# Query transposes of pairs 9 to 33 moved from DMA to TensorE, the last batch's first-half exponentials allowed behind stage A, and new planner constants

## The chip, the cores and the metric

The kernel runs on one core of one Trainium2 chip. A core has five engines with a queue each: TensorE (PE), VectorE (DVE), ScalarE (ACT), GpSimd (POOL) and SyncE (SP, which here issues nearly all DMAs). The metric is device time in microseconds (us); the time of a kernel is the median of several executions. PE rows come in pairs in the profile: PE is the matmul, PEld the load of its weights.

## The reference, cut to what matters

Stage A is attention with a soft cap, for 8 batches, 12 heads, 448 rows and head size 64. Stage B takes its output, heads side by side, as x (768 wide) and runs causal attention with four experts of head size 64, of which each row uses the two with the larger gate.

```python
scores = cap * tanh((q @ k.T) / sqrt(64) / cap)          # stage A, per head
x      = softmax(scores) @ v                             # 448 x 64, 12 heads -> 448 x 768
logits = x @ w_gate                                      # stage B, per batch
for e in range(4):
    a = softmax(causal((x @ wq[e]) @ (x @ wk[e]).T / sqrt(64)))
    out += weight_of_e_in_top_two * ((a @ (x @ wv[e])) @ wo[e])
```

## The kernel before, in words

**Tiling.** Two heads of a batch make a pair; there are 48 pairs, six to a batch. The key axis is cut into three chunks of 128 (one per head) and a shared chunk that holds the last 64 keys of both heads, so a pair has seven score tiles of 128 keys by 448 queries. The pairs of the last batch (42 to 47) are cut in two halves of 256 and 192 queries, and all first halves come before all second halves; together there are 54 "pieces".

**Stage A, per pair.** SP issues the loads of q, k and v for two pairs at a time into four rotating staging buffers (`load_part`, L271 to L297); a load into a buffer waits for the casts that read it last. POOL casts to 16-bit (`cast`, L342). q and k are then transposed so that the head size lies on the partitions. For pairs 0 to 8 PE does this with matmuls against an identity into PSUM (`a_tr`, L388) and DVE copies the result to the tile `qk` (`a_trev`, L408). From pair `FIRST_D` = 9 on, SP issues two DMA transposes instead, one of q and one of k (`a_trd`, L417, the DMA at L423). The DMA leaves q's columns in another order than the PE path, which `a_fill` (L482) undoes when it reads q, with the test `p >= FIRST_D` at L491. PE "fills" score tiles (L494), ACT takes their tanh into `y` (L505) and then the exponential of a whole piece into `pbuf` (L514). PE multiplies by v (`a_pv`, L518 to L535), DVE divides by the row sums (L541, L542), PE transposes the output (L555), and DVE copies it to `xT` (L568).

**Stage B, per batch.** When six pairs of `xT` are there: the projections of v and the gate (L612), with DVE copies that wait for a POOL memset of two columns of `vs` (L621); the projections of q and k (L716); the gate's masks on DVE and POOL; the score fills (L735) and their exponential on ACT (L742); the causal masks on POOL (L750); the product with v (L771) and its scaling (L789); a transpose (L807) and the output projection (L824). DVE copies its result to `ob` (L838) and SP stores it (L847). There are two `ob` buffers, so a copy can wait for the store of two tiles before. For the last batch (7) stage B is done by halves (`add_last`, L1152): the first half as soon as the first-half pieces are through (fills L1017, exponential `p0L` L1024), the second half at the very end (`tX` L946, fills L1055 to L1066, exponentials L1073 and L1077, output `lwo` L1145).

**Order.** Every engine executes in program order, and that order is made when the kernel is built, by a planner (`Sched`, L24). Each unit of work has an engine, a planned duration, dependencies and a due time; at each step the planner takes the unit that can start first and, among those close together, the one due first (`pick`, L122). A DMA also has a planned landing: `land` bytes at 2.15e5 bytes per us behind the DMAs before it (L107). Stage A's fills and ACT's operations have an order of their own (`next_fill`, L1427): the next fill is taken when a score buffer comes free (there are two, of three and two PSUM banks), and other PE units are put ahead of it if they end in time. `PV` shifts the due time of the P·V units, `TB` that of a batch's stage B, `T0D` that of the last batch's first half. Three further PSUM banks are shared by everything else (`NAUX` = 3). A stage B exponential ("X") takes a score buffer in turn when its inputs are planned to be ready; for the last batch, L1446 holds the last piece's fill back until both X of that batch are placed.

Of the kernel before, what the change touches and what calls it, by code (L numbers as in the profile page):

```python
# [14 lines left out]

DEBUG = False
NAUX = 3
PV = (7.0, 3.5, 0.0)
TB = (4.0, 4.0)
PACE = (1.0, 1.0)  # L20
T0D = 3.0


class Sched:  # L24
# [158 lines left out]
def kernel(  # L183
# [26 lines left out]
    TL = S - KM  # L210
    HALF = 256
    FIRST_D = 9

    WIN = (0, 128, 256, S - 128)
    VW = E * Dh + 2
# [81 lines left out]
            eng.dma_start(t[64 * g : 64 * (g + 1), g : 2 * n : 2, KC, :], s[g])  # L297

    def nbytes(n, which):
        return 2 * n * Dh * 4 * {"q": S, "k": KM, "v": KM}.get(which, TL // 2)  # L300

    ld_of = {}
    FIRST = [
# [6 lines left out]

    def add_load(p, n, w, due, e, deps):
        add(
            ("ld", w, p), e, 0.52, deps, due, load_part, p, n, w,
            nc.scalar if e == "ACT" else nc.sync, land=nbytes(n, w),
        )
        for i in range(n):
            ld_of[p + i, w] = ("ld", w, p)
# [87 lines left out]

    a_tr.ps, a_tr.t = {}, {}

    def a_trev(p, what):  # L408
        if p not in qkt:
            t = hd.tile([128, 1024], f16, name=f"qk_{p}", tag="qk", bufs=8)  # L410
            qkt[p] = (t[:, 0:S], t[:, S : S + 512])
            a_tr.t[p] = t
        lo, hi = {"qk": (0, S + 512), "q": (0, S), "k": (S, S + KM), "t": (S + KM, S + 512)}[what]
        cp = nc.scalar.copy if what == "k" else nc.vector.tensor_copy
        cp(a_tr.t[p][:, lo:hi], a_tr.ps.pop((p, what))[:, lo:hi])

    def a_trd(p, what):  # L417
        if p not in qkt:
            t = hd.tile([128, 1024], f16, name=f"qk_{p}", tag="qk", bufs=8)
            qkt[p] = (t[:, 0:S], t[:, S : S + 512])  # L420
        t = qkt[p][0 if what == "q" else 1]
        src = c16.pop(("q", p)) if what == "q" else c16["k", p]
        nc.sync.dma_start_transpose(  # L423
            out=t.rearrange("x (c p) -> x c p", c=4), in_=src.rearrange("p c h d -> p (c h d)")
        )

    def add_tr(p):
        deps = [("cast", w, p) for w in "qk"]
        if p >= 8:
            deps += [("filled", i) for i in of[p - 8]]  # L430
        due = nomp(p) - (8.0 if p > 3 else 3.5)
        if p == 0:
            for w, d in (("k", "k"), ("q", "q"), ("t", "kt")):
                add(("tr" + w, p), "PE", 0.14 * len(w), [("cast", d, p), ("ident",)], due, a_tr, p,
                    w, take=("tr" + w, p), slack=0.0)
                add(("trev" + w, p), "ACT" if w == "k" else "DVE", 0.4, [("tr" + w, p)], -50.0,
                    a_trev, p, w, give=("tr" + w, p))
            add(("trev", p), "-", 0.0, [("trevk", p), ("trevq", p)], -50.0, lambda: None)
            add(("tr", p), "-", 0.0, [("trt", p)], -50.0, lambda: None)
            return  # L440
        if p >= FIRST_D:
            due -= 6.0
            for w in "qk":
                add(("trd" + w, p), "SP", 1.2, [("cast", w, p)] + deps[2:], due, a_trd, p, w,
                    land=160000)
            add(("trev", p), "-", 0.0, [("trdq", p), ("trdk", p)], 0.0, lambda: None)
            add(("tr", p), "-", 0.0, [("trev", p)], 0.0, lambda: None)
            return
        add(("tr", p), "PE", 0.42, deps + [("ident",)], due, a_tr, p, take=("tr", p))
        add(("trev", p), "DVE", 0.58, [("tr", p)], due + 0.5, a_trev, p, "qk", give=("tr", p))  # L450
# [31 lines left out]
    def a_fill(i, slots, sc, tails):  # L482
        p, lo, n = pieces[i]
        qt, kk = qkt[p]
        for at, g, c in slots:
            if (c == KC) != tails:
                continue
            o = sc[:, at, 0:S] if n == S else sc[:, at // 2, at % 2 * 256 : at % 2 * 256 + n]
            r = slice(0, 128) if c == KC else slice(64 * g, 64 * g + 64)
            qs = qt[r, lo : lo + n]  # L490
            if p >= FIRST_D:  # L491
                o = o.rearrange("p (m c t) -> p m c t", c=QC, t=16)
                qs = qt[r, :].rearrange("p (c m t) -> p m c t", c=QC, t=16)[:, lo // 64 : (lo + n) // 64]
            nc.tensor.matmul(o, kk[r, 128 * c : 128 * (c + 1)], qs, start=True, stop=True)  # L494
# [75 lines left out]
    def add_pv(i):  # L570
        p, lo, n = pieces[i]
        b, j = divmod(p, HP)
        last = i == NK - 1
        due = -1000.0 if last else nom[i] + (PV[0] if n == S else PV[1] if lo == 0 else PV[2])
        for u in groups(i):
            for m in range(2):
                d = [("E", i), ("cast", "v", p)]
                d += [("pv", i, u, 0)] if m else []
                d += [("xt", i - 4)] if i >= 4 else []
                add(  # L580
                    ("pv", i, u, m), "PE", 0.26, d, due, a_pv, i, u, m,
                    take=("pv", i, u) if m == 0 else None, slack=0.05,
                )
            add(
                ("pvev", i, u), "DVE", 0.55, [("pv", i, u, 1)], due, a_pvev, i, u,
                give=("pv", i, u),
            )
        d = [("pvev", i, u) for u in groups(i)] + [("perm",)]
        add(("xt", i), "PE", 0.058 * 2 * len(groups(i)), d, due + 1.0, a_xt, i, take=("xt", i),
            slack=0.05 if last else None)  # L590
        d = [("xt", i)]
        if b >= 2:
            d += [("proj", b - 2)]
        add(("xtev", i), "DVE", 0.3 if n == S else 0.2, d, due + 1.0, a_xtev, i, give=("xt", i),
            alt=True)
# [255 lines left out]
    def add_wo(b, n, due, deps):  # L851
        if b < LB:
            deps = deps + stores[-2:-1]
        for f in range(2):
            add(("wo", b, n, f), "PE", 0.34, deps, due, b_wo, b, n, f, take=("wo", b, n, f))
            d = [("wo", b, n, f)]
            add(("woev", b, n, f), "DVE", 0.47, d, due + 0.5, b_woev, b, n, f,
                give=("wo", b, n, f), alt=True)
        add(
            ("st", b, n), "SP", 0.5, [("woev", b, n, 0), ("woev", b, n, 1)], due, b_store, b, n, 0,  # L860
            2, nc.sync, land=1 << 17,
        )
        if b < LB:
            stores.append(("st", b, n))
# [287 lines left out]
    def add_last():  # L1152
# [56 lines left out]
        for j in range(NDC):  # L1209
            for r in range(2):  # L1210
                for w in "qk":
# [1 line left out]
                    d += [("lqk", 1, r, w, j - 1)] if j else []  # L1213
                    d += [("lqk", 1, r, "q", 0)] if w == "k" and j == 0 else []
                    add(
                        ("lqk", 1, r, w, j), "PE", 0.085, d, c + r if j == NDC - 1 else tE - 1.0,
                        l_qk, 1, r, w, j, j + 1, slack=0.05,
                    )
        for r in range(2):
# [7 lines left out]
        for r in range(2):  # L1227
            for i in (1, 0):
                d = [("lqkev", 1, r, w) for w in "qk"] + [("T", NK - 1, 1), ("lqkev", 0, r, "k")]
                if r == 1 and i == 0:  # L1230
                    d += [("lqkev", 1, rr, w) for w in "qk" for rr in range(2)]
                add(
# [16 lines left out]
        for n in (2, 3):  # L1249
# [6 lines left out]
            for f in range(2):  # L1256
# [2 lines left out]
                add(("woev", b, n, f), eng, 0.5, d, c + n, b_woev, b, n, f, f == 1)  # L1259
                add(  # L1260
                    ("st", b, n, f), "SP" if f == 0 else "ACT", 0.4, [("woev", b, n, f)], c + n,
                    b_store, b, n, f, f + 1, nc.sync if f == 0 else nc.scalar, land=1 << 16,
                )

    tail_par = {}
# [161 lines left out]
    def next_fill():  # L1427
        nf, i = state["nf"], state["piece"]
        if i >= NK:
            sch.next_fill = None  # L1430
            return None
        r, armed = tile_free(nf)
        t = max(r, sch.free["PE"])
        if state["x"]:
# [1 line left out]
            d = x_deps(*x)  # L1436
            dur = 0.2 if x[0] == LB else 0.88
            if all(k in sch.done and sch.done[k][0] + 0.2 <= t for k in d) and (
                t + dur + 0.2 <= sch.act_ahead() or i >= NK - 1
                or t > max(sch.done[k][0] for k in d) + 6.0  # L1440
            ):
                return dict(r=r, dur=dur, armed=armed, special=True, go=lambda s: go_x(x, s, dur))
        p, lo, n = pieces[i]
        if ("trev", p) not in sch.done:
            return None
        if i == NK - 1 and info[i]["reads"] == 0 and state["x"]:  # L1446
            return None
        r = max(r, sch.done["trev", p][0] + 0.05)
        one = dict(r=r, dur=0.4, armed=armed, special=True, go=lambda s: go_t([i], s))
        if nf < 1 or n < S or not info[i]["rem"]:  # L1450
            return one
        nxt = pairs_of(i, 1)
        if nxt is None or pieces[nxt[0]][2] < S:
            return one
        r2, armed2 = tile_free(nf + 1)
        r2 = max(r2, nxt[1])
        two = dict(
            r=max(r, r2), dur=0.75, armed=armed and armed2, special=True,
            go=lambda s: go_t([i, nxt[0]], s),
        )  # L1460
        if r2 <= max(r, sch.free["PE"]) + 0.05:
            return two
        if max(r, r2) + 0.75 + sch.LAT["PE"] + 0.25 <= sch.act_ahead():
            return two
        return one

    def tile_of(par):
        return ps_score.tile(
# [143 lines left out]
```

## Time and profile before

| what | us |
|---|---|
| median of 11 runs | 337.95 (335.53 to 342.45) |
| the profiled execution, its own time | 342.45 |
| its span, first to last instruction | 340.7 |
| ACT busy | 293.8 |
| PE busy (ends modelled) | 275.7 |
| DVE busy | 200.4 |
| POOL busy | 174.2 |
| SP: 39 DMA transposes of q and 39 of k, issue of one (median) | 1.23 and 1.22 |
| stores of `ob`, issue to landing (median) | 2.7 |

The profile is of one execution, the slowest of the eleven. Rows name a line, an engine, an operation and its tiles (out<-in). In the list of waits a row says which engine and line sat idle, for which work, for how long in all, how often, and the longest. A timeline row has the start, the time taken, the engine and line, the tiles, how many instructions are merged in it and, in brackets, the idle time of the engine before it and what ended it. SPq is SP issuing a DMA. Busy shares are averages over stages with different limits, so idle time is read where it falls. PEclk is the granted clock of PE, as a part of full speed.

### The profile page before, as it was taken

To read this page: it belongs to the slowest core of one execution; us is meant where nothing else is said; L and a number is where in the kernel's file an instruction comes from. 1 tells how busy PE (TensorE), PEld (TensorE's weight loads), DVE (VectorE), ACT (ScalarE), POOL (GpSimd) and SP (SyncE) were. 2 spreads that over 40 slices of the span, in tenths; PEclk is the share of its full clock that TensorE was granted. 3 is DMA by queue.
4 is the path that set the end of the run, shared out by engine and by line. 5 is a ranking of instruction groups with operands and counts; after the bars stand their busy time and mean duration, and the time that the engine had idled before them with its cause. 6 is when DMAs were issued, how large, how long until landed. Compare 5 with 4: busy or idle time off the path is not lost.

```text
span 340.7 us, 8025 instructions
## 1 busy us (share of the span) xinstructions
PE 275.7 (81%) x3019; PEld 174.8 (51%) x3019; DVE 200.4 (59%) x643; ACT 293.8 (86%) x247; POOL 174.2 (51%) x346
## 2 busy tenths in 40 slices
PE   6767769977699759886799878887879979998972
PEld 2445445654456425454556545454545655576741
DVE  3453325767275835758367374747656647766873
ACT  4899978999799996998689989997988999994661
POOL 5796584895259631964419824673406421074110
PEclk9596769999999998999879999999989999999999
DMA  6999999959899688779799997877762000300035
GB/s 165 251 208 237 236 215 193 194 127 191 207 234 170 159 242 213 153 204 206 190 226 174 188 252 211 223 144 200 187 189 54 2 0 16 133 17 3 18 139 170
DMA packets 105191, 55.74 MB, mean 164 GB/s; under 512 B 65792, under 2 KB 101760, under 8 KB 105152
## 3 DMA queue, kind: packets, MB, share of 16 engines
q1 hardware_dynamic: 93888, 53.06, 67.7%
q0 software_dynamic: 10512, 1.58, 6.8%
q10 hardware_dynamic: 752, 0.59, 0.7%
q8 instruction: 24, 0.39, 0.5%
q14 instruction: 15, 0.12, 0.2%
HBM read 36.19 MB, written 11.01 MB: 139 GB/s over the span
## 4 chain that ended last, share of the span: by engine, by line
DMA 30%; PE 24%; POOL 11%; SPq 10%; DVE 9%; ACT 8%; issue 6%; POOLq 0%; DVEq 0%; ACTq 0%
DMA kst<-in_k_dram 10%; DMA vst<-in_v_dram 7%; DMA qf<-in_q_dram 7%; DMA out_dram<-ob 5%; PE sc L494 5%; PE vps L612 4%; SPq L297 3%; SPq L423 3%; ACT pbuf L514 3%; ACT y L505 3%; PE pv L532 3%; POOL k L351 2%; DVE ob L838 2%; PE wops L824 2%; SPq L288 2%
## 5 line engine op out<-in xcount | busy, mean ns | idle before, releaser
L505 ACT ACTIVATE y<-sc 128x896 f16<-128x896 f32 (+3 forms) x150 | 144.2, 1031 | 24.9 <-PE sc L494 24.4
L514 ACT ACTIVATE pbuf<-y 128x3136 f16<-128x3136 f16 (+2 forms) x54 | 137.8, 2551 | 0.2 <-PE pv L532 0.2
L494 PE MATMUL sc<-qk 64*128 64x448 f16 (+5 forms) x378 | 67.7, 360 | 5.3 <-ACT y L505 3.2
L532 PE MATMUL pv<-v,pbuf 128*128 128x65 f16 x1152 | 63.3, 198 | 0.0
L527 PE MATMUL pv<-v,pbuf 128*128 128x130 f16 x192 | 44.2, 230 | 23.3 <-ACT pbuf L514 13.4
L532 PEld LDWEIGHTS <-pbuf 128*128 128x128 f16 x1152 | 55.1, 101 | 5.1 <-issue 2.6
L347 POOL CAST q<-qf 112x512 f16<-112x512 f32 x46 | 28.3, 615 | 46.8 <-DMA qf<-in_q_dram 35.2
L542 DVE TENSOR_TENSOR xk<-pv,rc 128x256 f16<-128x256 f32 x96 | 40.8, 425 | 3.3
L838 DVE COPY ob<-wops 128x384 f32<-128x384 f32 (+1 forms) x56 | 29.5, 555 | 21.8 <-DMA out_dram<-ob 14.9
L494 PEld LDWEIGHTS <-qk 64*128 64x128 f16 (+1 forms) x378 | 20.3, 95 | 40.4 <-issue 32.3
L357 POOL CAST v<-vst 128x512 f16<-128x512 f32 x48 | 29.2, 619 | 21.5 <-PE pv L532 15.9
L527 PEld LDWEIGHTS <-pbuf 128*128 128x128 f16 x192 | 19.2, 100 | 34.2 <-ACT pbuf L514 18.7
L541 DVE RECIPROCAL rc<-pv 128x4 f32<-128x4 f32 x96 | 17.1, 178 | 27.7 <-PE pv L532 26.9
L824 PE MATMUL wops<-wo,oT 128*128 128x384 f16 x120 | 28.3, 341 | 5.6 <-DVE ob L838 3.4
L660 POOL COPY mb<-mk 128x1024 f16<-128x1024 f16 x14 | 14.2, 1041 | 34.1 <-DVE mk L655 34.1
L612 PE MATMUL vps<-wvg,xT 128*128 128x260 f16 x168 | 30.2, 292 | 1.8 <-DVE ob L838 1.8
L351 POOL CAST k<-kst 128x512 f16<-128x512 f32 x46 | 28.2, 616 | 4.6 <-DMA kst<-in_k_dram 3.7
L568 DVE COPY xT<-xtp 128x448 f16<-128x448 f16 (+2 forms) x52 | 18.8, 364 | 13.8 <-PE xtp L555 13.7
L716 PE MATMUL kps<-xT,wk 128*128 128x448 f16 x84 | 22.4, 353 | 1.8 <-DVE ob L838 1.5
L555 PE MATMUL xtp<-perm,xk 128*128 128x128 f16 x144 | 18.5, 227 | 5.8 <-DVE xk L542 2.6
L750 POOL TENSOR_SCALAR_AFFINE_SELECT pS<-pS 128x128 f16<-128x128 f16 (+1 forms) x56 | 14.6, 281 | 14.7 <-ACT pS L742 13.3
L716 PE MATMUL qps<-xT,wq 128*128 128x448 f16 x84 | 21.9, 358 | 0.1
(164 smaller groups left out, 406.2 us busy)
## 6 DMA issues: line engine op xcount, KB each, us to landing
qf<-in_q_dram SPq DMA_DIRECT2D x22, 448.0 KB, 5.9
vst<-in_v_dram SPq DMA_DIRECT2D x23, 384.0 KB, 5.0
out_dram<-ob SPq DMA_DIRECT2D x23, 384.0 KB, 2.7
kst<-in_k_dram SPq DMA_DIRECT2D x22, 384.0 KB, 4.3
out_dram<-ob SPq DMA_DIRECT2D x8, 192.0 KB, 2.7
kst<-in_k_dram SPq DMA_DIRECT2D x47, 32.0 KB, 4.9
vst<-in_v_dram SPq DMA_DIRECT2D x47, 32.0 KB, 4.6
kst<-in_k_dram SPq DMA_DIRECT2D x4, 192.0 KB, 4.1
```

Source lines behind the costliest of these rows:

```text
L351: cp(c16["k", p][:, 0:n], src.rearrange("p h c d -> p c h d")[:, 0:n])
L357: cp(v16[p % NV][:, :, :, 0:Dh], src)
L494: nc.tensor.matmul(o, kk[r, 128 * c : 128 * (c + 1)], qs, start=True, stop=True)
L505: nc.scalar.activation(ytile[i][:, first : first + nb, :], src, AF.Tanh, scale=isc / capf)
L514: nc.scalar.activation(ptile[i], ytile.pop(i), AF.Exp, scale=capf)
L527: nc.tensor.matmul(pv[:, n, :, :], ptile[i][:, idx[0, KC], w : w + 128], v16[p % NV][:, :, KC, :], start=(n == 0), stop=False, skip_group_ ...
L532: nc.tensor.matmul(pv[:, n, g, :], ptile[i][:, idx[g, c], w : w + 128], v16[p % NV][:, g, c, :], start=False, stop=(c == KC - 1), skip_gro ...
L542: nc.vector.tensor_tensor(xk, pv[:, :, :, 0:Dh], rc.broadcast_to((128, 2, 2, Dh)), ALU.mult)
L612: nc.tensor.matmul(ps, xT[b][:, j, w : w + 128], wvg[:, j, :], start=(j == 0), stop=(j == NDC - 1),)
L716: nc.tensor.matmul(s[which, r], w2[r][:, j, :], xT[b][:, j, :], start=(j == 0), stop=(j == NDC - 1),)
L824: nc.tensor.matmul(ps, s["oT"][:, r, w : w + 128], wo2[r][:, f * (D // 2) : (f + 1) * (D // 2)], start=(r == 0), stop=(r == 1),)
L838: cp(s["ob", n][lo:128, f * (D // 2) : (f + 1) * (D // 2)], s.pop(("wops", n, f))[lo:128, :],)
```

## The change

1. A second bound, `FIRST_Q` = 34, is added. For pairs 9 to 33 only k is transposed by DMA; q is transposed by four PE matmuls into a shared PSUM bank and copied to `qk` by DVE. From pair 34 on both go by DMA as before. `a_fill` undoes the column order from pair 34 on.
2. The planner's numbers: loads, transposes and stores get other planned landing times (a load's issue 0.62 instead of 0.52, a store's landing 1.2 instead of 0.61 us); `PV`, `TB` and `T0D` change; the last three pieces' P·V comes first of all (`LATE`).
3. The last batch's two first-half exponentials may follow stage A: the hold at L1446 goes, an X that wasn't placed by the end is added by `late_x` behind the last piece, and the second-half fills wait for both X. The second-half projections `lqk` get due times by chunk.
4. Two fills of half pieces (`n < S`) may be joined in one step, as those of whole pieces were.

```diff
-PV = (7.0, 3.5, 0.0)
-TB = (4.0, 4.0)
+PV = (9.0, 5.0, 2.0)
+TB = (0.0, 0.0)
 PACE = (1.0, 1.0)
-T0D = 3.0
+LATE = 3
+T0D = -4.0
...
     FIRST_D = 9
+    FIRST_Q = 34
...
     def nbytes(n, which):
-        return 2 * n * Dh * 4 * {"q": S, "k": KM, "v": KM}.get(which, TL // 2)
+        t = {"q": 224 * 0.055, "k": 256 * 0.045, "v": 256 * 0.045}.get(which, 64 * 0.03)
+        return n * t / 16 * 2.15e5
...
-            ("ld", w, p), e, 0.52, deps, due, load_part, p, n, w,
+            ("ld", w, p), e, 0.62, deps, due, load_part, p, n, w,
...
         if p >= FIRST_D:
-            due -= 6.0
-            for w in "qk":
-                add(("trd" + w, p), "SP", 1.2, [("cast", w, p)] + deps[2:], due, a_trd, p, w,
-                    land=160000)
+            for w in "qk" if p >= FIRST_Q else "k":
+                add(("trd" + w, p), "SP", 1.2, [("cast", w, p)] + deps[2:], due - 6.0, a_trd, p, w,
+                    land=1.05 * 2.15e5)
+            if p < FIRST_Q:
+                add(("trq", p), "PE", 0.21, [("cast", "q", p)] + deps[2:], due, a_tr, p, "q",
+                    take=("trq", p))
+                add(("trdq", p), "DVE", 0.37, [("trq", p)], due + 0.5, a_trev, p, "q",
+                    give=("trq", p))
...
-            if p >= FIRST_D:
+            if p >= FIRST_Q:
                 o = o.rearrange("p (m c t) -> p m c t", c=QC, t=16)
...
-        due = -1000.0 if last else nom[i] + (PV[0] if n == S else PV[1] if lo == 0 else PV[2])
+        due = -1000.0 + i if i >= NK - LATE else nom[i] + (PV[0] if n == S else PV[1] if lo == 0 else PV[2])
...
-            2, nc.sync, land=1 << 17,
+            2, nc.sync, land=1.2 * 2.15e5,
...
-                        ("lqk", 1, r, w, j), "PE", 0.085, d, c + r if j == NDC - 1 else tE - 1.0,
+                        ("lqk", 1, r, w, j), "PE", 0.085, d, c + r if j == NDC - 1 else c + 20.0 + j,
...
                 d = [("lqkev", 1, r, w) for w in "qk"] + [("T", NK - 1, 1), ("lqkev", 0, r, "k")]
+                d += [("X", LB, rr) for rr in range(2)]
...
         if i >= NK:
             sch.next_fill = None
+            for x in state["x"]:
+                late_x(x[1])
+            state["x"] = []
             return None
...
-                t + dur + 0.2 <= sch.act_ahead() or i >= NK - 1
-                or t > max(sch.done[k][0] for k in d) + 6.0
+                t + dur + 0.2 <= sch.act_ahead() or t > max(sch.done[k][0] for k in d) + 6.0
...
-        if i == NK - 1 and info[i]["reads"] == 0 and state["x"]:
-            return None
...
-        if nf < 1 or n < S or not info[i]["rem"]:
+        if nf < 1 or (not info[i]["rem"] and n == S):
             return one
...
-        if nxt is None or pieces[nxt[0]][2] < S:
+        if nxt is None or pieces[nxt[0]][2] != n:
             return one
...
+        both = 0.75 if n == S else 0.2 + n / 600
...
+    def late_x(r):
+
+        d = x_deps(LB, r) + [("T", NK - 1, 1)] + [("X", LB, 0)] * r
+
+        def fill():
+            L["late", r] = ps_score.tile(
+                [128, CAPS[tail_par[1]], 512], f32, name=f"lx_{r}", tag=f"sc{tail_par[1]}"
+            )
+            l_fill0(r, L["late", r])
+
+        add(("lfx", r), "PE", 0.45, d, -3000.0, fill)
+        add(("X", LB, r), "ACT", 0.7, [("lfx", r)], -3000.0, lambda: l_exp0(r, L.pop(("late", r))))
```

More of the change, by code (lines that the diff above doesn't have):

```diff
@@ L406, with qk_tile @@
     a_tr.ps, a_tr.t = {}, {}
+    def qk_tile(p):
+        if p not in qkt:
+            t = a_tr.t[p] = hd.tile([128, 1024], f16, name=f"qk_{p}", tag="qk", bufs=8)
+            qkt[p] = (t[:, 0:S], t[:, S : S + 512])
+        return a_tr.t[p]
     def a_trev(p, what):
[L409 to L412, printed above, removed]
+        t = qk_tile(p)
         lo, hi = {"qk": (0, S + 512), "q": (0, S), "k": (S, S + KM), "t": (S + KM, S + 512)}[what]
         cp = nc.scalar.copy if what == "k" else nc.vector.tensor_copy
-        cp(a_tr.t[p][:, lo:hi], a_tr.ps.pop((p, what))[:, lo:hi])
+        cp(t[:, lo:hi], a_tr.ps.pop((p, what))[:, lo:hi])
     def a_trd(p, what):
-        if p not in qkt:
-            t = hd.tile([128, 1024], f16, name=f"qk_{p}", tag="qk", bufs=8)
-            qkt[p] = (t[:, 0:S], t[:, S : S + 512])
+        qk_tile(p)
         t = qkt[p][0 if what == "q" else 1]
@@ L1261, in add_last @@
                     ("st", b, n, f), "SP" if f == 0 else "ACT", 0.4, [("woev", b, n, f)], c + n,
[L1262 removed]
+                    b_store, b, n, f, f + 1, nc.sync if f == 0 else nc.scalar, land=0.6 * 2.15e5,
                 )
@@ L1456, in next_fill @@
         r2 = max(r2, nxt[1])
+        both = 0.75 if n == S else 0.2 + n / 600
         two = dict(
-            r=max(r, r2), dur=0.75, armed=armed and armed2, special=True,
+            r=max(r, r2), dur=both, armed=armed and armed2, special=True,
             go=lambda s: go_t([i, nxt[0]], s),
@@ L1462, in next_fill @@
             return two
-        if max(r, r2) + 0.75 + sch.LAT["PE"] + 0.25 <= sch.act_ahead():
+        if max(r, r2) + both + sch.LAT["PE"] + 0.25 <= sch.act_ahead():
             return two
         return one
+    def late_x(r):
[7 more added lines that the diff above has]
+        add(("X", LB, r), "ACT", 0.7, [("lfx", r)], -3000.0, lambda: l_exp0(r, L.pop(("late", r))))
     def tile_of(par):
```

## The prediction

> **What bounds the kernel now.** I read the page first (which engine is fullest, when), then the waits (what the fullest engine lacks), then ScalarE's timeline with its bracketed idle times, then the other engines around each of these.
>
> ```profile
> span 340.7 us, 8025 instructions
> PE 275.7 (81%) x3019; PEld 174.8 (51%) x3019; DVE 200.4 (59%) x643; ACT 293.8 (86%) x247; POOL 174.2 (51%) x346
> DMA  6999999959899688779799997877762000300035
> ```
>
> ACT is the fullest engine and its order is fixed, so its idle time before the last exponential is lost one for one. The waits say whom it lacks, and who is late behind that:
>
> ```profile
> ACT y L505 <- PE sc L494: 24.4, 20, 3.2
> DVE ob L838 <- DMA out_dram<-ob: 15.9, 10, 4.2
> DVE vs L623 <- POOL vs L621: 6.7, 4, 3.5
> ACT p0L L1024 <- PE sc L1017: 4.5, 1, 4.5
> ```
>
> ACT waits for PE's score fills, 24.4 us. The four before 47 us are 2.6 of it; the sixteen from 47 to 262 us are 21.8. Between 276.7 and 308.3 it never waits over 0.2 us; then come 4.47 us for the last batch's stage B fill (p0L). The largest of the sixteen shows the chain that repeats:
>
> ```profile
> 122.62 1.23 SPq L423 DMA_TRANSPOSE qk<-q  x1
> ...
> 123.95 0.51 SPq L847 DMA_DIRECT2D out_dram<-ob  x1
> ...
> 126.88 1.02 DVE L838 COPY ob<-wops 128x384 f32<-128x384 f32 x2 [3.65 <-DMA out_dram<-ob]
> ...
> 127.49 0.80 PE L824 MATMUL wops<-wo,oT 128*128 128x384 f16 x2 [2.83 <-DVE ob L838]
> ...
> 130.82 0.92 ACT L505 ACTIVATE y<-sc 128x896 f16<-128x896 f32 x1 [3.16 <-PE sc L494]
> ```
>
> A store queues on SP behind a transpose, DVE's next output copy waits for its landing, PE waits for DVE, and the fill behind that on PE is late. The stage table (stretch; busy time and count of PE, weight loads, DVE, ACT, POOL; granted clock, DMA share, GB/s) adds that PE's clock was halved just then:
>
> ```profile
> 127.40:130.80 3.40, 3.31 (x13) 1.54 (x13) 1.93 (x6) 0.25 (x1) 0.00 (x0) 0.50 0.61 118
> ```
>
> Sorted by what PE was held by: stores under DVE's ob copies 9.2 us (130.82, 154.55, 203.20, 233.10, 253.16); stage B's vs memset, which stands on POOL behind a q cast that waits for its load, 4.2 (92.46, 171.17); right after a half-clock stretch 3.7 (163.54, 177.63, 257.12, 260.31); PE simply full or still starting 4.8 (47.54, 54.56, 66.32, 142.47, 246.44).
>
> **What the Trainium skill says.** "TensorE: Matmul & The Clock Gate", Part 1: the clock is halved after an idle window of about 3.4 us, so a PE stall is paid again. The trace agrees: stretches of 3.4 us at 0.50 begin at 127.4, 161.6, 171.8 and 253.7, the first in the 2.83 us wait above. Same page, Part 2: matmuls stay in program order; so does the trace's PE, which lets the fill stand behind the output projection. "DMA: Bandwidth & Descriptors", "Issuing engines are not separate DMA queues": all DMAs share the 16 engines. So fewer transposes help loads and stores too; the trace shows a DMA share of 0.90 from 47 to 165 us and 0.83 from 165 to 262.
>
> **The change part by part.** (1) q of pairs 9 to 33: 25 DMA transposes leave SP, at 1225 ns of issue (median of 39) 30.6 us of that queue, and 25 x 112 x 512 x 2 bytes = 2.9 MB of traffic, at the 192 GB/s of that stretch about 15 us. PE and DVE take over; the row of pair 0 prices it:
>
> ```profile
> L395 PE MATMUL trq<-ident,q x4: 212/213/223, 4.9 to 5.1; 112*128 112x112 f16 x4
> L415 DVE COPY qk<-trq x1: 392/392/392, 5.3 to 5.3; 128x448 f16<-128x448 f16 x1
> ```
>
> 100 matmuls start about 55 ns apart: 25 x 0.22 = 5.5 us of PE (at most 25 x 0.37, the four at half clock at 44.68, = 9.3). DVE gets 25 x 0.392 = 9.8 us; it is 59% busy, so free unless one stands before a copy that PE waits for. PE is the one to pay: of 5.5 us I charge 1.5 to ACT (none if all fall in PE's idle time, all 5.5 if none do). No data is late by this: POOL's casts run 5 to 12 pairs (of about 5.5 us) ahead of use.
>
> (2) Planner numbers. Stores count 1.2 instead of 0.61 us, other landings are re-set; projection dues move 4 us earlier (TB), P·V's 2 us later (PV). This costs no instruction; it moves them. In the built order the output copies no longer straddle as many transposes. What it brings: of the 4.3 us of store stalls at 130.82 and 154.55, where the q transposes also leave, 3.5; of the 4.9 at 203.20 to 253.16, where SP still issues both transposes (pairs 34 on), half, 2.4; of the memset's 4.2, half, 2.1, as the casts ahead of it wait less for loads; of the clock's 3.7, 1.0; of the last 4.8, none. Sum 9.0, net of PE 7.5. Bounds: -6 (below) to 21.8.
>
> (3) Last batch. Now the last piece's fill is held back until both p0L fills are placed:
>
> ```profile
> 307.67 0.67 ACT L505 ACTIVATE y<-sc 128x576 f16<-128x576 f32 x1
> 312.82 1.52 ACT L1024 ACTIVATE p0L<-sc 128x768 f16<-128x768 f32 x2 [4.47 <-PE sc L1017]
> ```
>
> In the changed order the three last pieces run through and p0L follows the last exponential: its end moves from 318.05 by 4.47 + 1.42 to about 312.2. What moves behind it: two exponentials, affine selects, P·V, DVE's scaling, the transposes lot; and PE has lot and otS ahead of the last two P·V windows. After the last exponential: exponentials, gate and a copy 2.0, affine 0.8, P·V 0.35, DVE 0.95, lot 0.3, last P·V 0.6, DVE 0.65, transpose 0.3, copy 0.3 = 6.3 us, where before 318.05 to 322.68 was 4.6: minus 1.7. At the end:
>
> ```profile
> 334.28 1.03 DVE L838 COPY ob<-wops 64x384 f32<-64x384 f32 x2
> ...
> 336.32 0.56 DVE L838 COPY ob<-lwo 64x384 f32<-64x384 f32 x1 [1.01 <-DMA out_dram<-ob]
> ```
>
> These two copies, batch 6's last, now stand before the first lwo copy, in a hole of 0.58 us and the idle time before it, and that batch is ready some 5 us earlier: plus 1.6 (2.0 less 0.4 as ACT's two stores now follow both copies). Sum 5.9 - 1.7 + 1.6 = 5.8. Bounds: 3 (the hole isn't there, the chain is longer) to 8.
>
> (4) Joined half-piece fills, the wait of the second-half fills for p0L, the later lqk dues: nothing. ACT has no idle time at 276.7 to 308.3 to win, a joined fill of seven matmuls (0.5 to 0.7 us) hides under an exponential of 1.32 to 1.74; without that cover 12 x 0.3 = 3.6 us. The second-half fills wait for their own evictions, later than p0L.
>
> The sum against the profiled execution: span 340.7 - 7.5 - 5.8 = 327.4, its time 342.45 - 13.3 = 329.1. But that execution is 4.5 us above the median 337.95, and I take its excess to lie in those stalls: the main part scales by (21.8 - 4.5)/21.8 = 0.79 to 5.9. 337.95 - 5.9 - 5.8 = 326.
>
> **The rivals.** Only the tail pays: casts are pairs ahead, so the transposes were hidden; the stalls are the planner's ordering errors, and new ones replace the old. For it: sixteen different places, only two of them with a q transpose of pairs 9 to 33 just ahead of the store. Against: SP's share in the longest. 337.95 - 5.8 + 1 = 333. That includes the case that (1) does not do what it seems to.
>
> All goes: every stall from 47 us on, and the tail: 337.95 - 17.3 - 6 = 315. For it: ACT would then be at its floor; against: half-clock stretches after 3.4 us of low PE activity are not all due to stores.
>
> Slower: PE takes on a wait for POOL's casts. In the built order the transposes of pairs 9 to 13 stand in the same pair as their casts; the last old PE transpose shows the price:
>
> ```profile
> 44.68 0.37 PE L395 MATMUL tr<-ident,q 112*128 112x112 f16 x4 [3.02 <-POOL q L347]
> ```
>
> PE stood 3.02 us for a cast and ACT lost 1.90 at 47.54. My gain of 11.7 is gone when 6 of the 25 do that; at 10, 326 + 19 = 345. Against: later pairs stand 2 to 6 pairs behind their casts.
>
> No change: the tail pays and six stalls of 1 us come new, 338.
>
> **How the numbers follow.** Forecast 326 at 0.50 (its own range 320 to 331); only the tail, 333, 0.22; all goes, 315, 0.12; slower, 345, 0.10; no change, 338, 0.06. From these: faster by over 0.5% 0.84, within 0.5% 0.06, slower 0.10; 0.5%, 1.7 us, is about what a measurement of this kernel can tell from no change. The range 316 to 337 leaves out the slower case and part of the full recovery.
>
> **What would show it.** The wait of ACT for fills falls from 24.4 to 13 to 17 us, of DVE for out_dram from 15.9 to under 8; DMA share from 47 to 165 us from 0.90 to about 0.8; 39 rows of transposed q become 14; the 4.5 us before p0L vanish; the last exponential ends 20 to 30 us before the span's end. It is wrong if PE waits on POOL q casts for over 5 us after 47 us, or if ACT's sum stays above 22.

## The result, and the profile after

The changed kernel takes 331.87 us (median of 12 runs, 329.41 to 336.32), the kernel before 337.88 (47 runs). The ratio is 0.9819 with a 95% interval of 0.9789 to 0.9848: 6.0 us or 1.8% faster. Medians are of all runs; a ratio compares only those runs of a kernel, and of the kernel before run beside it, that lie within 1.5% of the fastest of their kind, so the two can differ by some tenths of a per cent. The forecast was 326, that is 11.9 us less than before. The profiled execution of the changed kernel took 330.57 us, its span is 328.9. That is 11.8 us less than the span of before, but the execution profiled before lay 4.5 us above its median and this one lies 1.3 us below its own. The two traces therefore show twice what the medians show; below they say where time went, and the medians say how much.

The head of the page of the changed kernel (span; busy time, share and instructions of each engine):

```profile
span 328.9 us, 8178 instructions
PE 278.3 (85%) x3119; PEld 178.5 (54%) x3119; DVE 208.0 (63%) x667; ACT 293.0 (89%) x248; POOL 173.9 (53%) x346
```

ACT is still the fullest engine, with nearly the same busy time (293.8 before), now 89% of a shorter span. The waits (who waited for whom; us in all, times, longest):

```profile
POOL q L350 <- DMA qf<-in_q_dram: 27.7, 8, 8.6
ACT y L513 <- PE sc L502: 15.1, 12, 6.0
...
DVE vs L631 <- POOL vs L629: 6.3, 1, 6.3
```

ACT's wait for fills fell from 24.4 to 15.1 us. DVE's wait for stores, 15.9 before, is no longer in the list. The wait of 4.5 us before `p0L` is gone too. Added up by stage, ACT's bracketed waits for fills are:

| stage, us | before | after |
|---|---|---|
| start to 47 | 2.6 | 5.1 |
| 47 to 75 | 4.0 | 8.5 |
| 75 to 262 | 17.8 | 1.6 |

From 75 us on nearly everything is won, and before 75 us 7.0 us are lost. The stages by engine, first before, then after (stretch; busy time and count of PE, weight loads, DVE, ACT, POOL; clock, DMA share, GB/s):

```profile
47.00:75.00 28.00, 25.66 (x266) 15.68 (x265) 16.14 (x54) 25.40 (x20) 20.80 (x40) 0.90 1.02 177
75.00:165.00 90.00, 71.56 (x808) 45.88 (x806) 55.79 (x168) 81.54 (x61) 50.19 (x91) 0.96 0.86 197
165.00:262.00 97.00, 80.92 (x848) 49.36 (x846) 59.01 (x186) 87.39 (x65) 47.67 (x85) 0.96 0.83 191
```

```profile
47.00:75.00 28.00, 21.77 (x223) 13.84 (x222) 12.65 (x43) 19.49 (x15) 16.82 (x26) 0.82 1.15 215
75.00:165.00 90.00, 80.41 (x958) 52.07 (x956) 63.20 (x200) 89.20 (x67) 56.42 (x108) 1.00 0.81 194
165.00:262.00 97.00, 88.56 (x1015) 56.77 (x1016) 68.20 (x211) 96.21 (x73) 52.08 (x99) 1.00 0.62 152
```

From 75 us on ACT is now busy for 89.2 of 90 and 96.2 of 97 us, and PE's clock shows 1.00. Between 47 and 75 us ACT is busy for only 19.5 of 28 us, where it was 25.4. One stall makes most of that, here in the timeline of the changed kernel:

```profile
47.60 0.98 SPq L281 DMA_DIRECT2D qf<-in_q_dram  x1
...
57.89 0.62 POOL L350 CAST q<-qf 112x512 f16<-112x512 f32 x1 [5.49 <-DMA qf<-in_q_dram]
...
59.70 0.12 POOL L629 MEMSET vs<- 128x6 f16 x1
...
60.43 0.27 PE L535 MATMUL pv<-v,pbuf 128*128 128x130 f16 x1 [5.61 <-DVE vs L631]
...
61.62 0.92 ACT L513 ACTIVATE y<-sc 128x896 f16<-128x896 f32 x1 [5.97 <-PE sc L502]
```

A load of q lands 10 us after its issue. POOL, in order, stands at the cast of it, stage B's memset stands behind the cast, DVE behind the memset, PE behind DVE, and the fill behind that. This is the chain that the prediction listed for 92.46 and 171.17; it is now at 61.62 and costs 6 us at once.

At the end, the last exponential of stage A now ends at 301.66, and 27.2 us follow it; before it ended at 318.1, with 22.6 us behind it. The timeline of the changed kernel, and below it the last transpose (xtp) of before:

```profile
300.34 1.32 ACT L522 ACTIVATE pbuf<-y 128x1344 f16<-128x1344 f16 x1
...
311.12 0.22 PE L563 MATMUL xtp<-perm,xk 128*128 128x128 f16 x1
```

```profile
322.05 0.22 PE L555 MATMUL xtp<-perm,xk 128*128 128x128 f16 x1
```

The last transpose of stage A's output (xtp) starts 9.5 us after the last exponential; before it started 3.9 us after. In between PE and DVE do stage B's work for batch 6 and for the last batch's first half: P·V, transposes and output projections.

### The profile page after: what moved, and what is told of

The parts are those of the page before. It is cut to its first block, busy times and chain, and to the rows that moved or that the text cites. A ratio compares the mean times of both kernels' runs of the same rounds, so it can differ in the third digit from the quotient of the medians.

```text
span 328.9 us, 8178 instructions
## 1 busy us (share of the span) xinstructions
PE 278.3 (85%) x3119; PEld 178.5 (54%) x3119; DVE 208.0 (63%) x667; ACT 293.0 (89%) x248; POOL 173.9 (53%) x346
## 4 chain that ended last, share of the span: by engine, by line
PE 38%; ACT 23%; DVE 16%; DMA 14%; issue 4%; POOL 2%; SPq 2%; DVEq 0%; ACTq 0%; POOLq 0%
ACT y L513 10%; ACT pbuf L522 10%; DMA vst<-in_v_dram 8%; PE sc L502 7%; PE pv L540 4%; PE wops L832 4%; PE sc L743 4%; PE vps L620 4%; PE qps L724 3%; DMA wvg<-in_moe_wv_dram 3%; DVE o L797 3%; PE pv L535 2%; PE kps L724 2%; ACT pS L750 2%; DMA qf<-in_q_dram 2%
## 5 line engine op out<-in xcount | busy, mean ns | idle before, releaser
L513 ACT ACTIVATE y<-sc 128x896 f16<-128x896 f32 (+3 forms) x150 | 143.8, 1043 | 15.4 <-PE sc L502 15.1
L502 PE MATMUL sc<-qk 64*128 64x448 f16 (+4 forms) x378 | 64.3, 352 | 7.1 <-ACT y L513 5.6
L540 PE MATMUL pv<-v,pbuf 128*128 128x65 f16 x1152 | 61.9, 198 | 0.0
L350 POOL CAST q<-qf 112x512 f16<-112x512 f32 x46 | 28.3, 619 | 27.8 <-DMA qf<-in_q_dram 27.7
L502 PEld LDWEIGHTS <-qk 64*128 64x128 f16 (+1 forms) x378 | 19.5, 94 | 42.8 <-issue 36.6
L549 DVE RECIPROCAL rc<-pv 128x4 f32<-128x4 f32 x96 | 17.1, 178 | 23.5 <-PE pv L540 22.8
L846 DVE COPY ob<-wops 128x384 f32<-128x384 f32 (+1 forms) x55 | 28.8, 553 | 4.0 <-PE wops L832 3.4
L576 DVE COPY xT<-xtp 128x448 f16<-128x448 f16 (+2 forms) x51 | 18.3, 366 | 19.5 <-PE xtp L563 19.4
L620 PE MATMUL vps<-wvg,xT 128*128 128x260 f16 x168 | 28.7, 280 | 0.0
L832 PE MATMUL wops<-wo,oT 128*128 128x384 f16 x120 | 27.2, 332 | 0.9 <-DVE ob L846 0.2
L724 PE MATMUL qps<-xT,wq 128*128 128x448 f16 x84 | 23.3, 359 | 0.1
L620 PEld LDWEIGHTS <-xT 128*128 128x128 f16 x168 | 15.8, 99 | 10.7 <-issue 3.9
L682 POOL TENSOR_TENSOR ee<-euler,lg 128x16 f32<-128x16 f32 x7 | 20.4, 2916 | 0.0
```

What stands on the lines that cost most here:

```text
L350: cp(c16["q", p], src.rearrange("p h (c d) -> p c h d", c=QC))
L513: nc.scalar.activation(ytile[i][:, first : first + nb, :], src, AF.Tanh, scale=isc / capf)
L540: nc.tensor.matmul(pv[:, n, g, :], ptile[i][:, idx[g, c], w : w + 128], v16[p % NV][:, g, c, :], start=False, stop=(c == KC - 1), skip_gro ...
L620: nc.tensor.matmul(ps, xT[b][:, j, w : w + 128], wvg[:, j, :], start=(j == 0), stop=(j == NDC - 1),)
L724: nc.tensor.matmul(s[which, r], w2[r][:, j, :], xT[b][:, j, :], start=(j == 0), stop=(j == NDC - 1),)
L832: nc.tensor.matmul(ps, s["oT"][:, r, w : w + 128], wo2[r][:, f * (D // 2) : (f + 1) * (D // 2)], start=(r == 0), stop=(r == 1),)
```

## The experiments

Each ratio is against the kernel before, run beside it on the same chip; its median there was 336.9 to 338.7 us. Parts (1) the q split, (2) the planner's numbers, (3) the last batch (with the joined fills (4)) were run in all eight combinations:

| (1) | (2) | (3) | median, us | ratio to before, 95% |
|---|---|---|---|---|
| | | | 337.88 | 1 |
| x | | | 323.86 | 0.959 (0.954 to 0.964) |
| | x | | 335.62 | 0.986 (0.981 to 0.991) |
| | | x | 343.01 | 1.015 (1.010 to 1.019) |
| x | x | | 332.61 | 0.988 (0.983 to 0.992) |
| x | | x | 329.24 | 0.975 (0.971 to 0.979) |
| | x | x | 331.04 | 0.983 (0.979 to 0.987) |
| x | x | x | 331.87 | 0.982 (0.979 to 0.985) |

### Part (1) alone

```diff
+    FIRST_Q = 34
...
-            for w in "qk":
+            for w in "qk" if p >= FIRST_Q else "k":
...
+            if p < FIRST_Q:
+                add(("trq", p), "PE", 0.21, [("cast", "q", p)] + deps[2:], due, a_tr, p, "q",
```

> The kernel before with part (1) alone: q of pairs 9 to 33 transposed by PE, all planner numbers and the last batch as before. Theory A, that of the prediction (SP's queue and the DMA engines are relieved where the stores and loads are late): 25 transposes of 1.23 us leave SP, the store stalls shrink by 2 to 4 us, PE costs 1.5, so 0.5 to 3 us faster, 335 to 337. Theory B (the stalls are ordering errors of the planner's numbers, and q's transposes were hidden): 0 to 2 us slower, 338 to 340, with DVE's wait for out_dram still above 10 us. If it is over 4 us faster, the DMA side alone carries the whole gain.

323.86 us, 14 us faster, and 8 us faster than the whole change. First POOL's wait for loads of q before, then three waits of this kernel:

```profile
POOL q L347 <- DMA qf<-in_q_dram: 35.2, 11, 8.0
```

```profile
POOL q L348 <- DMA qf<-in_q_dram: 11.9, 7, 2.9
...
ACT y L511 <- PE sc L500: 9.3, 9, 3.1
...
DVE ob L844 <- DMA out_dram<-ob: 0.3, 1, 0.3
```

The wait of POOL for loads of q, 35.2 us before, falls to a third, and the waits for stores are gone with it, though no planned number of a store was touched. Theory A has the direction; its size, 0.5 to 3 us, was far too small, and the case of the last sentence came true.

### Part (2) alone

```diff
-PV = (7.0, 3.5, 0.0)
-TB = (4.0, 4.0)
+PV = (9.0, 5.0, 2.0)
+TB = (0.0, 0.0)
...
-            2, nc.sync, land=1 << 17,
+            2, nc.sync, land=1.2 * 2.15e5,
```

> The kernel before with part (2) alone: the planned landings, the load's issue of 0.62 us, PV and TB; both transposes by DMA from pair 9 on. Theory A: about half of the main gain, 2.5 to 4 us faster, 334 to 335.5. Theory B: the whole main gain, 5 us or more faster, under 333, DVE's wait for out_dram under 6 us. If it is within 1 us of the kernel before, the numbers are worth something only where the queue has been relieved (the parts need each other).

335.62 us, 1.4% faster by the ratio and 0.9% by the medians (338.65 us for the kernel before beside it), near theory A's time. The numbers also clear the stretch from 75 to 262 us: 4.2 us of ACT's waits there in place of 17.8. But they bring the early stall, 6.33 us at 59.19. So the two parts win largely the same stalls, and only this one brings the early stall.

### Part (3) alone

```diff
-T0D = 3.0
+LATE = 3
+T0D = -4.0
...
-        if i == NK - 1 and info[i]["reads"] == 0 and state["x"]:
-            return None
```

> The kernel before with part (3) and (4) alone: the two first-half exponentials of the last batch may follow stage A, joined half fills, due times of the last pieces. Theory A (the prediction): 5.8 us faster, 332. Theory C: the last exponential of stage A ends 5 us or more earlier, but the stretch behind it gets as much longer, since the same work of PE, DVE and ACT has still to be done there: within 1.5 us of the kernel before, with 4 us or more added between the last exponential and the end.

343.01 us, 1.5% slower. The last exponential ends at 312.37 in place of 318.1, as forecast; but the stretch behind it is 31.0 us in place of 22.6. The last of stage A's output transposes starts at 320.76, 8.4 us after the exponential (9.5 in the whole change).

Theory C holds for the end, and even it was too mild.

### Four output buffers, order unchanged

```diff
-    outp = ctx.enter_context(tc.tile_pool(name="outp", bufs=2))
+    outp = ctx.enter_context(tc.tile_pool(name="outp", bufs=4))
...
-                [128, D], f32, name=f"ob_{b}_{n}", tag="obL" if b == LB else "ob"
+                [128, D], f32, name=f"ob_{b}_{n}", tag="ob"
```

> The kernel before in its own order, every engine's instructions unchanged, with four output buffers shared by all batches instead of two and two: only the wait of DVE's output copies for the store of two tiles before is taken away. If the 9.2 us of stalls that the trace puts under these waits are their work alone: DVE's wait for out_dram falls from 15.9 to under 2 us, ACT's wait for fills from 24 to 15 or 16, 6 to 9 us faster, 329 to 332. If another late thing stands right behind them (loads on the same queue, PE's half clock): under 3 us faster, 335 to 338.

338.51 us, ratio 1.000 (0.997 to 1.003). In the traces every engine's instructions come in the same order as before. The waits for stores are gone, and nothing is won. The waits of this kernel:

```profile
POOL q L347 <- DMA qf<-in_q_dram: 47.8, 13, 7.7
ACT y L505 <- PE sc L494: 22.3, 17, 5.9
```

What PE no longer waits for at the stores it waits for at POOL's casts: POOL's wait for q rises from 35.2 to 47.8 us, and ACT has stalls of 4.64 us at 168.67 and 5.93 at 245.98. Behind both stands a cast of q that waited for its load (5.62 us at 165.65, 7.73 at 237.84). The 9.2 us that the prediction put under stores can't be won at the stores: with the order unchanged, the late loads of q take their place.

### The whole without one part

Without (1):

```diff
-    FIRST_Q = 34
+    FIRST_Q = 9
```

> The changed kernel without part (1): both transposes by DMA from pair 9 on, the planner's numbers and the last batch as changed. Theory A (the prediction's sum, in which the q split nets 2 of the 11.7 us): 2 to 4 us slower than the changed kernel, 334 to 336. Theory D (the q split carries the gain through the loads, the numbers alone gave 1.4% and the last batch's order took 1.5% away): 336 to 341, POOL's wait for the load of q back at 30 us or more.

331.04 us: no slower than the whole. Without the split POOL waits 29.6 us for q, with it 27.7; the early stall is there, 6.42 us at 59.78. With all the numbers of (2) in, the split is worth nothing, which neither theory expected.

Without (2):

```diff
-PV = (9.0, 5.0, 2.0)
-TB = (0.0, 0.0)
+PV = (7.0, 3.5, 0.0)
+TB = (4.0, 4.0)
...
-            2, nc.sync, land=1.2 * 2.15e5,
+            2, nc.sync, land=1 << 17,
```

> The changed kernel without part (2): q split and the last batch as changed, the old planned landings, PV and TB. The q split alone ran 323.9. Theory D1 (the last batch's order is what the whole change loses): the stretch behind stage A's last exponential is again 27 us or more where the q split alone had 22, so 328 to 332. Theory D2 (the planner's numbers lose it, by the vs memset that they set behind a late q cast): 323 to 326, and no stall over 4 us before 70 us.

329.24 us. Against the split alone, part (3) adds 5 us here; the stretch behind the last exponential is 31.7 us in place of 22.0. No wait of ACT for fills is over 4 us. D1 holds.

Without (3) and (4):

```diff
-LATE = 3
-T0D = -4.0
+T0D = 3.0
...
+        if i == NK - 1 and info[i]["reads"] == 0 and state["x"]:
+            return None
```

> The changed kernel without parts (3) and (4): q split and planner numbers. Theory D1: 323 to 325, a tail of about 22 us behind the last exponential. Theory D2: the stall of about 6 us at 60 us is there as in the changed kernel, so 327 to 330. Both at once: 326 to 328 here and about 328 without the numbers.

332.61 us: the numbers cost about 9 us when they are added to the split. The stall is at 60.98, 5.30 us, and `p0L` is held back again for 4.53. D2 holds too, and more strongly than expected. Between this kernel and the whole change, part (3) shows no difference beyond the intervals. In the traces it lengthens the stretch behind the last exponential by 8.4 us (on the kernel before) and 9.7 (on the split) with the old numbers, but by 3.5 (without the split) and 4.2 (with it) with the new ones. Which of the numbers does that was not tried.

### The memset moved to DVE

```diff
-            nc.gpsimd.memset(s["vs"][:, :, 0 : VW : VW - 1], 1.0)
+            nc.vector.memset(s["vs"][:, :, 0 : VW : VW - 1], 1.0)
```

> The changed kernel with one instruction moved: the memset of two columns of vs, once per batch, is done by DVE instead of POOL, so it no longer stands behind POOL's casts (DVE pays seven memsets of about 0.1 us). If the 5.97 us stall at 61.6 us is this memset's: it goes, ACT's wait for fills falls from 15 to about 9 us, 5 to 6 us faster than the changed kernel, 326 to 327. If the late q load holds PE anyway, by the next transposes of q: at most 2 us faster, 330 to 332, with a stall of 3 us or more between 55 and 70 us that names POOL's q cast.

328.30 us, ratio 0.975 (0.970 to 0.979); the changed kernel has 0.982 (0.979 to 0.985). This lies between the two expectations. The stall at 61.6 is gone and one of 6.12 us stands at 73.63, so that ACT's waits for fills hardly fall (14.3 us in place of 15.1). The timeline of this kernel:

```profile
60.13 0.62 POOL L350 CAST q<-qf 112x512 f16<-112x512 f32 x1 [6.60 <-DMA qf<-in_q_dram]
...
67.88 2.02 POOL L668 COPY mb<-mk 128x1024 f16<-128x1024 f16 x2
...
68.98 0.50 PE L705 MATMUL mps<-ident,mb 128*128 128x128 f16 x3 [4.71 <-POOL mb L668]
...
73.63 0.92 ACT L513 ACTIVATE y<-sc 128x896 f16<-128x896 f32 x1 [6.12 <-PE sc L502]
```

The next thing behind the late casts on POOL, the gate's masks, takes the memset's place. The same move on top of the split alone:

> The kernel with the q split alone, and the memset of two columns of vs moved from POOL to DVE. In the split alone this memset stands behind a late q cast once, 3.17 us, with a stall of 3.09 us at 55.25. If the memset is its cause: 320 to 322. If the late load only passes the wait on to what stands next on POOL, as moving it in the changed kernel did: 323 to 324, the same stall some 10 us later.

323.45 us against 323.86, with ratios of 0.960 and 0.959: no difference. The time is that of the second expectation, the trace is not: the stall of 3.09 us at 55.25 is gone, and no wait of ACT for fills before 262 us is longer than 1.9 us, so none came in its place. Its worth, 1.5 us between the two spans, can't be told from the scatter of these runs.

### The q transposes issued again, their result unused

On top of the split alone, SP issues the 25 DMA transposes of q again, into tiles that nobody reads:

```diff
+                add(("trs", p), "SP", 1.2, [("cast", "q", p)] + deps[2:], due - 6.0, a_trs, p,
+                    land=160000)
...
+        nc.sync.dma_start_transpose(
+            out=scr[i % 6].rearrange("x (c p) -> x c p", c=4),
```

> The kernel with the q split alone (323.9), and on top of it the 25 DMA transposes of q are issued by SP again, into a scratch tile that nobody reads: PE and DVE still make the q that is used. SP's issue time, its waits for POOL's casts and the DMA traffic are those of the kernel before; only the fills no longer wait for the DMA's result. Theory A (the split helps because SP and the DMA engines are relieved, so that loads and stores come in time): back to 333 or more. Theory F (it helps because of the order that the planner builds with it, or because the fills no longer hang on a DMA): 322 to 327.

337.87 us, ratio 0.997 (0.993 to 1.000): the whole gain of the split is gone, while the fills still take q from PE.

```profile
POOL q L348 <- DMA qf<-in_q_dram: 30.1, 12, 8.0
ACT y L528 <- PE sc L517: 21.0, 21, 3.3
```

So the transposes cost 14 us though no instruction waits for their result. How they do it is not shown by this run alone, for the planner plans them too: it still sets a pair's fills behind their planned landing, and the order of PE, DVE and POOL goes back towards that of before. The first four memsets of `vs` stand on POOL behind 11, 19, 26 and 33 casts of q before, behind 11, 19, 26 and 34 here, and behind 11, 20, 29 and 36 with the split alone. The part of theory F that puts the gain down to the order stays open.

SP shows how little room there was. The durations of SP's DMA rows that start between 75 and 165 us add up to 83.0 us of 90 before (63 plain ones 41.6, 32 transposes 41.4), 83.5 here, and 72.6 with the split alone. A transpose also stands on SP until its cast is done. SP's own waits, before:

```profile
SPq L423 <- POOL k L351: 13.0, 12, 1.7
SPq L423 <- POOL q L347: 10.8, 11, 1.5
```

The Trainium skill, "DMA: Bandwidth & Descriptors", the section "Anatomy of one DMA — SWDGE (gpsimd) path", says that DMA engines don't wait on semaphores: the wait happens at the issuing engine before dispatch. The trace agrees: the transposes' waits for casts are SP's, and the loads for the next casts stand behind them. But a full SP alone doesn't cost the time. With part (2) alone its rows fill 82.5 of the same 90 us, and POOL's waits for loads of q from 75 to 262 us are 29.7 us, 30.2 before; yet ACT waits for fills only 4.2 us there, 17.8 before. So the order, which sets what stands behind a late cast, decides how much of POOL's wait reaches ACT.

Nor do the loads themselves take much longer. Those of q issued between 75 and 165 us landed after 5.5 us before, 5.1 with the split alone and 5.1 here (medians); but there are 8, 10 and 8 of them, so with the split they are issued closer together. That speaks against the 2.9 MB of traffic as the main cause. SP's issue time, its waits and the order were not separated.

### Which of the planner's numbers costs

The split alone with the new planned landings and the load's issue of 0.62 us, but the old `PV` and `TB`:

```diff
+        t = {"q": 224 * 0.055, "k": 256 * 0.045, "v": 256 * 0.045}.get(which, 64 * 0.03)
+        return n * t / 16 * 2.15e5
...
+            ("ld", w, p), e, 0.62, deps, due, load_part, p, n, w,
```

> The kernel with the q split alone, and of the planner's numbers only the planned landings and the load's issue of 0.62 us; PV and TB stay as before. The split with all numbers ran 8.7 us slower than the split alone. Theory L (the landings do it: loads are planned to land earlier than they do, POOL's casts of q are set too early, and what stands behind them on POOL is late): 329 to 333, with a stall of 4 us or more between 50 and 75 us. Theory T (TB does it: stage B of a batch is set 4 us earlier and meets the late loads): 323 to 325, no such stall.

331.61 us, with a stall of 4.78 us at 62.95: the landings (or the load's issue) do it. Then the split with all the new numbers, and only the planned bytes of a load as before:

```diff
     def nbytes(n, which):
-        t = {"q": 224 * 0.055, "k": 256 * 0.045, "v": 256 * 0.045}.get(which, 64 * 0.03)
-        return n * t / 16 * 2.15e5
+        return 2 * n * Dh * 4 * {"q": S, "k": KM, "v": KM}.get(which, TL // 2)
```

> The q split with all of the planner's new numbers (that ran 332.6) except one function: a load's planned bytes are again those of the kernel before (448 KB for two pairs of q, 2.13 us planned, instead of 1.54 us). Theory N (the load's planned landing of 1.54 us, which asks for 298 GB/s where the trace moved 200 to 271 GB/s with full DMA engines, is what sets POOL's casts too early): 322 to 326, no stall over 4 us between 40 and 75 us. Theory O (another of the numbers, the load's issue of 0.62 us, the store's or the transpose's landing, or TB): 329 to 333 with the stall still there.

322.19 us, ratio 0.958 (0.952 to 0.963): faster than both kernels, by 4.2% and, from the two ratios, 2.5%. Its waits:

```profile
POOL q L348 <- DMA qf<-in_q_dram: 6.5, 4, 2.2
ACT y L511 <- PE sc L500: 5.0, 8, 1.1
```

No wait of ACT for fills before 262 us is longer than 1.13 us. One function of two lines was worth 10 us, against 332.61 with its new form. The other new numbers then add nothing to the split that these runs can tell (0.958 and 0.959).

Two pairs of q are 458,752 bytes. The new formula plans 2 x 224 x 0.055 / 16 = 1.54 us for their transfer, which is 298 GB/s for this load alone; the loads of k and v get shorter plans too. In the stage of the stall the changed kernel moved 215 GB/s with full DMA engines (share 1.15). At the old rate of 2.15e5 bytes per us the same load is planned with 2.13 us. That is still short of the trace, in which a load of q took up to 11.2 us from issue to landing, but it changes POOL's order. In all five kernels with the new formula and the memset on POOL, 13 casts of q stand on POOL ahead of the first memset of `vs`. Here it is 12, and the memset is through before the cast that waits:

```profile
50.83 0.12 POOL L627 MEMSET vs<- 128x6 f16 x1
...
55.19 0.61 POOL L348 CAST q<-qf 112x512 f16<-112x512 f32 x1 [1.65 <-DMA qf<-in_q_dram]
```

Planned to land too early, the cast is put too early into POOL's order, and everything behind it waits.

## Why the prediction was right, and where it was not

**Right in sign, half the size, and in the range by luck.** The time lies in the range, and it is nearest to the rival "only the tail pays", 333. That rival's reason is wrong, however: by the ratios the tail brought at most a little, and parts (1) and (2) the rest. From the ratios, (1) and (2) together gave 1.2%, 4.2 us (forecast 5.9 at the median). Adding (3) and (4) gave 0.6%, 1.8 us, which the intervals don't tell from nothing (forecast 5.8). Taken step by step, the split brought 12 us more than its 2.0, the numbers on top of it 15 less than their 5.5, and the tail 4 less: large errors that nearly cancel.

**Step (1), the q split: a large error.** The prediction gave it 3.5 us of store stalls less 1.5 of PE. Alone it is worth 14. The price of PE was not the error: in the changed kernel PE waits 0.3 us for casts of q at its transposes after 47 us. The mechanism, fewer transposes on SP, has the right direction, since issuing them again takes all back; whether the queue or the order built for it carries the gain is open. The error was the sorting of the stalls. What PE was held by (stores, memset, half clock) was read as four causes with a price each, but the run with four output buffers shows that the first gives way to the next: casts of q that wait for their loads. The longest wait in the list of before, POOL's for `qf`, was the one that the prediction did not show. "No data is late by this" was true of the casts ahead of use, and missed what else stands behind a cast on POOL.

**Step (2), the planner's numbers.** Counted at 2.4 for stores, 2.1 for the memset and 1.0 for the clock, without a cost. Alone they clear 13.6 of ACT's 17.8 us after 75 us, more than that. The bound "-6 (below)" was meant for PE's waits; the loss came in another place: the planned landings of loads bring a stall of 4.8 to 6.4 us between 59 and 63 us in every kernel that has them and keeps the memset on POOL. The prediction read "other landings are re-set" and priced it at nothing; it did not compare the planned rate with the GB/s of the stage table. It expected that casts would wait less for loads; the 4.2 us that ACT lost behind the memset became 6.0 in one stall.

**The sum.** (1) and (2) were added. They do not add: 4.1% and 1.4% alone, 1.2% together.

**The noise step.** The excess of 4.5 us of the profiled execution was spread over the stalls by a factor of 0.79. The forecast for that execution, 329.1, is close to the 330.57 that was profiled, but the difference between the traces is 5.8 us larger than between the medians. Taken off whole, the excess would have left 13.3 - 4.5 = 8.8 us of gain, nearer to the 6.0.

**Step (3), the last batch.** The last exponential came earlier by the hold and the two `p0L`, as forecast. The chain behind it to the last copy of `xT` was put at 6.3 us, 1.7 more than before. It took 10.1 (301.66 to 311.72), so the step was short by 3.8. The end was to win 1.6; from that copy to the end it is 17.1 us in place of 18.1, so about 0.9. Net, 5.9 - 5.5 + 0.9 = 1.3 in the traces, not 5.8. The sum counted one chain with its own durations, as if PE and DVE were free for it. They had the first half's output to do in the same microseconds. Which of the queued pieces holds the last transposes was not tried.

**Step (4)** and the second-half dues were not run apart from (3).

**What would show it.** ACT's wait of 13 to 17 us (15.1), the wait for stores under 8 (gone), 14 rows of transposed q, the vanished 4.5 us and an end 27.2 us behind the last exponential came as said. Neither sign of being wrong came: 0.3 us of PE's waits, and 15.1 us of ACT's. The DMA share from 47 to 165 us did not fall to 0.8 (0.90 before, 0.89 after): from 75 to 165 us it fell from 0.86 to 0.81, but from 47 to 75 us it rose from 1.02 to 1.15.

## What to carry to other kernels

When several engines take turns in being the last wait, don't add up the waits: take one of them away with the order unchanged, and see whether the time moves. Look for the wait that the engines pass on in order (here POOL's for a load), for what stands behind it in the program, and for the queue that feeds it (SP's issue rows filled 92% of a stage). The wait alone says little: with part (2) alone POOL waited as long after 75 us as before, and ACT hardly lost anything there. In a kernel with a planned order, a planned transfer rate above what the trace moved puts consumers too early, and they block what stands behind them.

## What the runs showed that was not expected

A small thing in the tail of the changed kernel:

```profile
305.60 1.15 POOL L805 TENSOR_TENSOR o<-o 128x512 f16<-128x512 f16 x1 [1.16 <-DVE rcL L1118]
305.64 1.13 DVE L1120 TENSOR_TENSOR slL<-rcL,wtokL 128x4 f32<-128x4 f32 x1
```

A product of four columns took 1.13 us on DVE, and 0.16 in its other three places; it ends with POOL's addition. The Trainium skill, "GPSIMD Engine Reference", section "Specifications", says that the SBUF interfaces of GpSimd are shared with VectorE, with contention for DVE instructions that have two SBUF inputs; this one has two. It is not the only one (count; shortest, median and longest in ns):

```profile
L793 DVE TENSOR_TENSOR cf<-wm,rcS x28: 166/166/647, 82.0 to 304.8; 128x6 f32<-128x6 f32 x28
L550 DVE TENSOR_TENSOR xk<-pv,rc x96: 423/425/426, 16.7 to 310.0; 128x256 f16<-128x256 f32 x96
```

The product `cf` also has both inputs in SBUF. The 15 that no POOL instruction overlaps take 166 to 169 ns, the 13 others a median of 395. The product `xk` reads `pv` from PSUM, and its 86 places beside POOL take 423 to 426 ns like the rest. The trace agrees with the page; no run tested it.
